# A first MLP whose products go ahead of its transposes, and three zero pieces sent at its end

## The chip, the cores and the metric

The kernel runs on one core of a Trainium2 chip. The metric is the device time of one execution, in microseconds. Engines are named as in the profile: PE (matrix products and transposes; PEld are its weight loads), DVE, ACT and POOL (vector, scalar and general work), SP (which issues most transfers). Sixteen DMA engines move data between the chip's large memory (HBM) and the on-chip memory.

## The reference

Two decoder layers for one token, forward and backward. A layer is an attention part (32 query heads on 4 key/value heads, the last 4096 positions of a cache of 32768) and an MLP with the Mish activation; both layers use the same weights. The result is the output and the gradients of x, both caches, wq, wo, w1, b1 and w2.

```python
x = x + _A_ref(_layernorm(x), k_cache, v_cache, wq, wo)   # A0
x = x + _B_ref(_layernorm(x), w1, b1, w2)                 # B0
x = x + _A_ref(_layernorm(x), k_cache, v_cache, wq, wo)   # A1
x = x + _B_ref(_layernorm(x), w1, b1, w2)                 # B1
# _A_ref: q = x @ wq; softmax(q k^T * Dh**-0.5) v; then @ wo
# _B_ref: h = x @ w1 + b1; act = h * tanh(softplus(h)); act @ w2
_out, _vjp = jax.vjp(_f, x, k_cache, v_cache, wq, wo, w1, b1, w2)
_grads = _vjp(grad_out)
```

Sizes: D = 1024, J = 4096 (wq's columns), F = 3584 (the MLP's width), everything in bf16. The gradients of the caches are zero except in the last 4096 positions, so 58.7 MB of plain zeros have to be written.

## The kernel before, in words

A token's vector lies as columns, 128 elements per column, so a matrix-vector product is a row of PE instructions with a 128x128 block of the weight as the stationary operand and a moving operand of one column. The weights don't fit on the chip at once and are read several times.

**The ring.** Weight chunks of 1 MB go through a ring of eight slots. `ring.want` writes down, in the order of the whole program, which chunk comes next; whenever a slot is released (`ring.release`, after its last reader), `pump` issues the next wanted load on SP (L71). Whoever releases a slot gets not his own next chunk but the next one in the list. In the first layers the list runs: wq, V, w2 chunks 0 and 1, wo, w1, w2 chunks 2 to 6, then wq pieces 0, 1, 2 for layer A1 (pieces 3 to 7 were kept from A0 and hold five slots), wo for A1, wq again, and so on. Chunk 3 of w2 has a home of its own: the tile `zt`.

**Zeros.** `zt` is later set to zero by POOL (L728) and then is the source of 56 zero pieces of 1 MB each, which `zeros(n, after)` issues on POOL's own DMA queue (L264). With `after` given, POOL first copies one element of that tensor (L259), so the pieces start no sooner than it is ready. The places of these calls spread the zeros over the program: nine in A1's forward part, the rest up to the last stage.

**The first MLP, B0** (from L716). After the products with w1 (L621) and the activation on DVE, a loop runs over the seven chunks of w2. `mlp_out` (L673) makes 32 products with AC, the activation. Beside this forward product, each chunk is used for the backward product of the last layer's gradient with w2 (into `da1`), since it is on the chip anyway. Its four blocks of 1024 columns go two ways: blocks 0 and 1 as row products on DVE (`rowdot`, L427; the vector `gbc` broadcast over the partitions), blocks 2 and 3 as `turned`: eight PE transposes into a PSUM buffer (L450), an eviction by ACT back over the block in the ring (L306), and then eight PE products with GB, here called GB products (L462). `later` keeps those back until the next `flush`, so the order on PE is: forward products of chunk c, GB products of chunk c-1, transposes of chunk c. Chunks 0 and 1 were already treated wholly by `rowdot` and are only released.

Chunk 6 has its turn in `last_da`, which is the `q_hook` of A1's `attn_fwd`: it is issued behind the layer norm and ahead of the query product (L493, eight pieces of wq with 32 products each, in the order 3, 4, 5, 6, 7, 0, 1, 2). Behind the query product stand the scores (L510) and the softmax.

**The last stage.** The backward part of A0 (`attn_bwd(0, ...)`) calls the hook `dn1(t)` after each of eight wq pieces. When it is over, the remaining output gradients are made as outer products and written (SP, L989 and L994).

Of the kernel before, what the change touches and what calls it, by code (L numbers as in the profile page):

```python
# [18 lines left out]
D = 1024  # L19
# [4 lines left out]
TD = D // P  # L24
TF = F // P
# [4 lines left out]
def scol(g, t):  # L30
    return ((t // 2) * 4 + g) * 16 + (t % 2) * 8
# [62 lines left out]
def kernel(  # L94
# [22 lines left out]
    nc = tc.nc  # L117
# [13 lines left out]
    def sb(shape, dtype, name):  # L131
        return keep.tile(shape, dtype, name=name)
# [3 lines left out]
    def tmp(shape, dtype, name):  # L136

        if name not in scratch:
            scratch[name] = keep.tile(shape, dtype, name=name)
        return scratch[name]  # L140
# [10 lines left out]
    gbc = DSX[:, 1024:2048]  # L151
# [11 lines left out]
    TP = psum.tile([P, 512], FP32, name="TP")  # L163
# [7 lines left out]
    def big():  # L171
        if wide:
            wide.append(wide.pop(0))
            return wide[-1][:, 0:512]
        b = bigs[big_n[0] % len(bigs)]
        big_n[0] += 1
        return b
# [16 lines left out]
    for hi in range(4):  # L194
        r = slice(32 * hi, 32 * hi + 32)
# [7 lines left out]
    GB = sb([P, TD, 2], BF16, "GB")  # L203
# [16 lines left out]
    ring = Ring(nc, [ring_t[:, i, :] for i in range(8)])  # L220
# [35 lines left out]
    def zeros(n, after=None):  # L256

        if after is not None and zjobs:
            nc.gpsimd.tensor_copy(pz[0:1, pz_n[0] % 16:pz_n[0] % 16 + 1], after[0:1, 0:1])  # L259
            pz_n[0] += 1  # L260
        for _ in range(n):
            if zjobs:
                dst = zjobs.pop()
                nc.gpsimd.dma_start(dst, zt[:])  # L264
# [32 lines left out]
    def evac(dst, src, eng=None, cost=(0.69, 1.0)):  # L297

        if eng is None:
            eng = "D" if load["D"] + cost[0] <= load["A"] + cost[1] else "A"  # L300
        if eng == "D":
            load["D"] += cost[0]
            nc.vector.tensor_copy(dst, src)  # L303
        else:
            load["A"] += cost[1]
            nc.scalar.copy(dst, src)  # L306
# [74 lines left out]
    def residual(y_ps, x, name):  # L381
        xn = sb([P, TD], FP32, f"x_{name}")
        st = tmp([P, 2], FP32, "st")
        junk = tmp([P, TD], FP32, "xx")
        nc.vector.scalar_tensor_tensor(out=xn[:], in0=y_ps, scalar=1.0, in1=x[:], op0=ALU.mult, op1=ALU.add,
                                       accum_out=st[:, 0:1])
        nc.vector.scalar_tensor_tensor(out=junk[:], in0=xn[:], scalar=1.0, in1=xn[:], op0=ALU.mult, op1=ALU.mult,
                                       accum_out=st[:, 1:2])
        return xn, st
# [30 lines left out]
    def rowdot(w, vecs, n, acc, fours=False):  # L420

        for i, vec in enumerate(vecs):
            out, a = junk[:, 0:n], w[:, i * n:(i + 1) * n]
            if fours:
                out, vec = (x.rearrange("a (k p) -> a k p", p=P) for x in (out, vec))
                a = a.rearrange("a (p k) -> a k p", k=4)
            nc.vector.tensor_tensor_reduce(out=out, in0=a, in1=vec, scale=1.0,  # L427
                                           scalar=acc if i else 0.0, op0=ALU.mult, op1=ALU.add, accum_out=acc)
        load["D"] += len(vecs) * (n * 1.1e-3 + 0.18)
# [4 lines left out]
    def later(f, product=False):  # L434

        lag.append((product, f))
        while sum(p for p, _ in lag) > behind[0]:
            lag.popleft()[1]()
        while lag and not lag[0][0]:
            lag.popleft()[1]()  # L440

    def flush():
        while lag:
            lag.popleft()[1]()

    def turned(w, n, mv, eng=None, block=None):

        b = big().bitcast(BF16)
        for i in range(n):
            nc.tensor.transpose(b[:, i * P:(i + 1) * P], block(w, i) if block else w[:, i * P:(i + 1) * P], ident_bf[:])  # L450
        evac(w, b[:, 0:n * P], eng, cost=(0.69 * n / 8, n / 8))
        later(mv, True)

    fresh = [False]

    def mv_open():

        fresh[0] = True

    def mv(w, n, out, rhs_of, last):  # L460
        for i in range(n):
            nc.tensor.matmul(out, lhsT=w[:, i * P:(i + 1) * P], rhs=rhs_of(i), start=fresh[0], stop=last and i == n - 1,  # L462
                             skip_group_check=True)
            fresh[0] = False

    def rows_chunk(ch, c, col, l, vec, dst, off, nr=2, eng="A"):

        for tt in range(4):
            r = 4 * c + tt
            if tt < nr:  # L470
                rowdot(ch[:, tt, :], [vec], D, dst[:, r:r + 1])
            else:
                w = ch[:, tt, :]
                turned(w, TD, lambda w=w, r=r: mv(w, TD, TP[:, off + r:off + r + 1], lambda i: col[:, i, l:l + 1], True), eng)
# [6 lines left out]
    def attn_fwd(l, x, st, first, wo_hook, q_hook=None):  # L481
# [2 lines left out]
        if first:  # L484
            kt_transposes()
        if q_hook is not None:
            q_hook()
        q_ps = MV[:, 0:HQ]
        order = list(range(TD)) if l == 0 else sorted(range(TD), key=lambda t: t not in KEEP_Q)
        for k, t in enumerate(order):  # L490
            ch = ring.get(("q", l, t))
            for h in range(HQ):
                nc.tensor.matmul(q_ps[:, h:h + 1], lhsT=ch[:, h * P:(h + 1) * P], rhs=NA[:, t, l:l + 1],  # L493
                                 start=(k == 0 and h == 0), stop=(k == TD - 1), skip_group_check=True)
            if l == 0 and t in KEEP_Q:
                ring.keep(("q", 0, t), ("q", 1, t))
            else:
                ring.release(("q", l, t))
        qv = QC[:].rearrange("p v (g u l h) -> p v g u l h", g=G, u=2, l=2)
        nc.vector.tensor_scalar(out=qv[:, 0, :, 0, l, :], in0=q_ps.rearrange("p (g h) -> p g h", g=G), scalar1=scale,  # L500
                                scalar2=None, op0=ALU.mult)
# [4 lines left out]
        for i in range(2):  # L506
            for t in range(16 * i, 16 * i + 16):
                for g in range(G):
                    c = scol(g, t) - 512 * i
# [30 lines left out]
        for i in range(2):  # L540
            nc.vector.reduce_sum(m64[i][:], EX[:, i * 512:(i + 1) * 512].rearrange("p (tp c) -> p c tp", c=64), axis=AX.X)
            for g in range(G):
                for t in range(16 * i, 16 * i + 16):
                    c = scol(g, t)
# [22 lines left out]
        y_ps = MV[:, 128:128 + TD]  # L567
        for c in range(8):
            ch = ring.get(("o", l, c))
# [99 lines left out]
    def mlp_out(l, ch, c, y_ps):  # L669
        for tt in range(4):  # L670
            fb = 4 * c + tt
            for dd in range(TD):
                nc.tensor.matmul(y_ps[:, dd:dd + 1], lhsT=ch[:, tt, dd * P:(dd + 1) * P], rhs=AC[:, fb, l:l + 1],  # L673
                                 start=(fb == 0 and dd == 0), stop=(fb == TF - 1), skip_group_check=True)
# [26 lines left out]
    da1 = tmp([P, HQ], FP32, "da")  # L701
    DA = 64
# [13 lines left out]
    mp0 = sB0["deriv"]()  # L716
    y_ps = MV[:, 256:256 + TD]
    mv_open()
    for c in range(7):
        ch = ring.get(("2", 0, c))  # L720
        mlp_out(0, ch, c, y_ps)
        flush()
        if c in EARLY_2:
            ring.release(("2", 0, c))
        elif c < 6:
            rows_chunk(ch, c, GB, 1, gbc, da1, DA)
            later(lambda c=c: ring.release(("2", 0, c)))
    nc.gpsimd.memset(zt[:], 0.0)  # L728
    x2, st2 = residual(y_ps, x1, "B0")


    def last_da():

        rows_chunk(ring.get(("2", 0, 6)), 6, GB, 1, gbc, da1, DA)
        flush()
        ring.release(("2", 0, 6))
        v = da1[:, 8:TF].rearrange("p (a b) -> p a b", b=4)[:, :, 2:4]
        nc.vector.tensor_copy(v, TP[:, DA + 8:DA + TF].rearrange("p (a b) -> p a b", b=4)[:, :, 2:4])

    def wo_hook1(c):  # L740
        if c == 0:
# [15 lines left out]
    def take_back(name, base, off):  # L757
        r = DR[name][:].rearrange("(n l) p -> l n p", l=2)
        nc.sync.dma_start(ROWS[base:base + 2, off:off + r.shape[1] * P].rearrange("l (n p) -> l n p", p=P), r)

    x3, st3, sA1 = attn_fwd(1, x2, st2, False, wo_hook1, last_da)
    put_by("OC", OC, HQ)
    put_by("NA", NA, TD)
# [9 lines left out]
    dnp = sb([P, TD], FP32, "dnp")  # L773
# [231 lines left out]
    def twins():  # L1005
        for base, n in ((96, NOFF + F), (64, NOFF + F), (32, NOFF + J), (0, NOFF + J)):
            nc.sync.dma_start(TWIN[base ^ 32:(base ^ 32) + 2, 0:n], ROWS[base:base + 2, 0:n])
# [26 lines left out]
    def units_cols(base, ncol, out):  # L1034

        for t in range(TD):
            s = stage_free.popleft()
            n = 0
            while n < ncol:
                m = unit_dw(base, t * P, NOFF + 512 * n, s[:, n * 512:ncol * 512], ncol - n)  # L1040
                n += m
                store(out[t * P:(t + 1) * P, :], s, n - m, n, ncol, t == TD - 1)
                yield
# [50 lines left out]
    y_ps = MV[:, 384:384 + TD]  # L1094
    mv_open()
    even()
    for c in range(7):
        ch = ring.get(("2", 1, c))
# [43 lines left out]
        zeros(4, DQC[:, 0, 0:1])  # L1142

    def dn1(t):
        if t in (3, 6, 7):
            zeros(2 if t == 3 else 1, dnp[:, t:t + 1])
        if t == 4:
            twins()
        if t == 5:
            todo[0].append(units_cols(0, 8, out_4))  # L1150
# [57 lines left out]
```

## Time and profile before

| what | value |
|---|---|
| median of 3 runs | 460.42 us (459.21 to 463.47) |
| profiled execution, its own time | 461.23 us |
| its span, first to last instruction | 459.2 us |
| PE busy | 341.7 us (74%) |
| DVE, ACT, POOL busy | 256.6 us (56%), 225.0 us (49%), 38.7 us (8%) |
| moved by DMA | 179.38 MB, 388 GB/s over the span |
| of it on SP's queue, on POOL's queue | 119.74 MB, 58.72 MB |
| mean granted PE clock | 0.629 |

The span is what the profile sees; the execution's own time adds what lies around it, 2.0 us. A PE instruction counts as busy for its whole length although instructions overlap, so a busy PE is not PE at its peak. The granted clock is a share of full speed; it is 0.50 or 1.0 in long stretches of this trace.

### The profile page before, as it was taken

The page shows a single profiled execution, that of the slowest core. Times are in us where ns is not written, and L with a number is a line of the kernel's source. Part 1 is how long each engine was busy: PE and PEld are TensorE (multiplying, and loading weights), DVE is VectorE, ACT ScalarE, POOL GpSimd, SP SyncE. Part 2 cuts the span into 40 slices and gives each one's busy share as a digit, 9 for nine tenths or more (in the row PEclk, how much of TensorE's full clock was granted, in tenths as well). Part 3 has the DMA queues.
Part 4 walks back from the last instruction along what each step waited for, and adds up shares of the span by engine and source line. Part 5 has one row for each costly group of instructions (what it writes and reads, how often), then busy time and mean ns, then how long its engine had stood idle before and what let it go on. Part 6 is the DMA issues. An engine that isn't in the chain of part 4 may idle for free. (4 is left out here: it accounts for less than half of the span.)

```text
span 459.2 us, 14200 instructions
## 1 busy us (share of the span) xinstructions
PE 341.7 (74%) x6361; PEld 276.6 (60%) x6361; DVE 256.6 (56%) x516; ACT 225.0 (49%) x261; POOL 38.7 (8%) x85
## 2 busy tenths in 40 slices
PE   3836445598679888598879798798797888889900
PEld 3735434497569887498779798697693222224600
DVE  4505731283060149677528676657456999998810
ACT  2502001055045379377317555157064999999900
POOL 1000000030103322200211000101221000000000
PEclk9955555555555569699759955589586555555555
DMA  8999999877999999999999988999999999999995
GB/s 337 421 420 418 418 419 416 361 278 261 385 425 422 421 417 418 415 399 415 420 422 418 421 320 298 347 344 368 422 419 424 412 422 422 418 421 416 405 407 213
DMA packets 27802, 179.38 MB, mean 391 GB/s; under 512 B 3642, under 2 KB 3670, under 8 KB 9430
## 3 DMA queue, kind: packets, MB, share of 16 engines
q1 hardware_dynamic: 19586, 119.74, 65.5%
q0 software_dynamic: 8064, 58.72, 30.9%
q8 instruction: 49, 0.80, 0.6%
q14 instruction: 11, 0.09, 0.0%
q10 hardware_dynamic: 92, 0.02, 0.0%
HBM read 79.74 MB, written 98.62 MB: 388 GB/s over the span
## 5 line engine op out<-in xcount | busy, mean ns | idle before, releaser
L306 ACT COPY ring<-BIG 128x1024 bf16<-128x1024 bf16 x62 | 60.7, 1014 | 41.5 <-PE BIG L450 36.1
L450 PE MATMUL BIG<-ident_bf,ring 128*128 128x128 bf16 x744 | 67.4, 255 | 1.8 <-ACT W L306 1.1
L450 PEld LDWEIGHTS <-ring 128*128 128x128 bf16 x816 | 61.5, 116 | 2.8 <-issue 2.2
L1015 PE MATMUL wide<-W 2*128 2x512 bf16 x228 | 52.1, 598 | 9.3 <-ACT W L306 2.0
L427 DVE CUSTOM_DVE_ANT_0 junk<-ring,SC 128x1024 bf16<-128x1024 bf16 x34 | 41.3, 1215 | 5.4 <-DMA ring<-in_B_w_dram 3.7
L1015 PEld LDWEIGHTS <-W 2*128 2x128 bf16 x240 | 12.6, 102 | 44.3 <-issue 43.2
L462 PEld LDWEIGHTS <-ring 128*128 128x128 bf16 x912 | 31.6, 98 | 9.3 <-ACT ring L306 6.7
L306 ACT COPY KT<-BIG 128x1024 bf16<-128x1024 bf16 x22 | 21.8, 1016 | 30.3 <-PE BIG L602 28.7
L303 DVE CAST ring<-wide 128x1024 bf16<-128x1024 f32 (+1 forms) x29 | 33.7, 1199 | 3.2 <-PE wide L1015 1.5
L306 ACT COPY W<-BIG 128x1024 bf16<-128x1024 bf16 x28 | 26.7, 1119 | 16.0 <-PE BIG L788 14.9
L306 ACT CAST ring<-wide 128x1024 bf16<-128x1024 f32 (+1 forms) x35 | 32.9, 1018 | 1.3 <-PE wide L1066 0.5
L303 DVE COPY ring<-BIG 128x1024 bf16<-128x1024 bf16 x31 | 21.3, 690 | 19.3 <-PE BIG L450 12.2
L264 POOL DMA_DIRECT2D out_dram<-zt x56 | 29.7, 534 | 22.9 <-DMA out_dram<-zt 22.0
L621 PE MATMUL MV<-NB,W 128*128 128x1 bf16 x448 | 16.2, 172 | 9.3 <-DMA W<-in_B_w_dram 6.5
L493 PE MATMUL MV<-NA,ring 128*128 128x1 bf16 x512 | 14.9, 165 | 11.0 <-DMA ring<-in_A_wq_dram 8.6
L621 PEld LDWEIGHTS <-W 128*128 128x128 bf16 x448 | 15.9, 118 | 9.8 <-DMA W<-in_B_w_dram 7.2
L303 DVE CAST VS<-wide 128x1024 bf16<-128x1024 f32 (+1 forms) x17 | 19.7, 1186 | 3.6 <-PE wide L1015 3.0
L1066 PE MATMUL wide<-W 32*128 32x256 bf16 x128 | 20.9, 402 | 0.9 <-ACT ring L306 0.8
L306 ACT CAST KT<-wide 128x1024 bf16<-128x1024 f32 x20 | 20.4, 1032 | 1.8 <-PE wide L1015 0.9
L493 PEld LDWEIGHTS <-ring 128*128 128x128 bf16 x512 | 14.2, 103 | 11.5 <-DMA ring<-in_A_wq_dram 9.1
L427 DVE CUSTOM_DVE_ANT_0 junk<-ring,DSX 128x1024 bf16<-128x1024 bf16 x16 | 19.6, 1224 | 1.1 <-DMA ring<-in_B_w_dram 0.7
L427 DVE CUSTOM_DVE_ANT_0 junk<-W,SC 128x512 bf16<-128x512 bf16 (+1 forms) x20 | 15.8, 791 | 6.5 <-PE SC L330 5.8
(268 smaller groups left out, 566.9 us busy)
## 6 DMA issues: line engine op xcount, KB each, us to landing
out_dram<-zt POOLq DMA_DIRECT2D x56, 1024.0 KB, 16.2
ring<-in_A_wq_dram SPq DMA_DIRECT2D x22, 1024.0 KB
ring<-in_A_wo_dram SPq DMA_DIRECT2D x14, 1024.0 KB
ring<-in_B_w_dram SPq DMA_DIRECT2D x13, 1024.0 KB
W<-in_A_wo_dram SPq DMA_DIRECT2D x10, 1024.0 KB
W<-in_B_w_dram SPq DMA_DIRECT2D x8, 896.0 KB
out_dram<-ring SPq DMA_DIRECT2D x7, 1024.0 KB
out_dram<-ring SPq DMA_DIRECT2D x13, 512.0 KB
```

The costliest lines, as they stand in the source:

```text
L264: nc.gpsimd.dma_start(dst, zt[:])
L303: nc.vector.tensor_copy(dst, src)
L306: nc.scalar.copy(dst, src)
L427: nc.vector.tensor_tensor_reduce(out=out, in0=a, in1=vec, scale=1.0, scalar=acc if i else 0.0, op0=ALU.mult, op1=ALU.add, accum_out=acc)
L450: nc.tensor.transpose(b[:, i * P:(i + 1) * P], block(w, i) if block else w[:, i * P:(i + 1) * P], ident_bf[:])
L462: nc.tensor.matmul(out, lhsT=w[:, i * P:(i + 1) * P], rhs=rhs_of(i), start=fresh[0], stop=last and i == n - 1, skip_group_check=True)
L493: nc.tensor.matmul(q_ps[:, h:h + 1], lhsT=ch[:, h * P:(h + 1) * P], rhs=NA[:, t, l:l + 1], start=(k == 0 and h == 0), stop=(k == TD - 1), ...
L621: nc.tensor.matmul(h_ps[:, fb:fb + 1], lhsT=f_block(W1[:, t], fb), rhs=NB[:, t, l:l + 1], start=(t == 0 and fb == 0), stop=(t == TD - 1), ...
L1015: nc.tensor.matmul(b[:, 512 * i:512 * i + 512], lhsT=R[at:at + 2, lo:lo + P], rhs=R[at:at + 2, ro + 512 * i:ro + 512 * i + 512], start=Tru ...
L1066: nc.tensor.matmul(b[:, k * 256:(k + 1) * 256], lhsT=RT[32 * g:32 * g + 32, a, tp, :], rhs=YS[32 * g:32 * g + 32, :], start=True, stop=Tru ...
```

## The change

In B0 the loop over the chunks is written out by hand. `turned` is split into `turn_pe` (the transposes) and `turn_ev` (the eviction), so that the two can stand at different places. The transposes of chunk 2 are issued ahead of the first forward products; evictions and GB products of a chunk follow later, with forward products of the next chunk between them. Chunk 5's and chunk 6's transposes, evictions and GB products move into the second query product: `q_hook` is now called with -1 ahead of it and with k behind each of its eight pieces, and `last_da` acts at -1, 1 and 3. Right behind the memset of `zt`, three zero pieces are issued on POOL. In the last stage `dn1` issues one piece instead of four: one at t = 3 instead of two, none at t = 6 and 7. The number of pieces, 56, and all arithmetic stay.

```diff
+    def turn_pe(w, n, block=None):
         b = big().bitcast(BF16)
         for i in range(n):
             nc.tensor.transpose(b[:, i * P:(i + 1) * P], block(w, i) if block else w[:, i * P:(i + 1) * P], ident_bf[:])
+        return b
+
+    def turn_ev(w, b, n, eng=None):
         evac(w, b[:, 0:n * P], eng, cost=(0.69 * n / 8, n / 8))
+
+    def turned(w, n, mv, eng=None, block=None):
+        turn_ev(w, turn_pe(w, n, block), n, eng)
         later(mv, True)
...
         if q_hook is not None:
-            q_hook()
+            q_hook(-1)
...
+            if q_hook is not None:
+                q_hook(k)
...
-    for c in range(7):
-        ch = ring.get(("2", 0, c))
-        mlp_out(0, ch, c, y_ps)
-        flush()
+    def da_out(c):
+        mlp_out(0, ring.get(("2", 0, c)), c, y_ps)
+    def da_dots(c):
+        ch = ring.get(("2", 0, c))
+        for tt in range(2):
+            rowdot(ch[:, tt, :], [gbc], D, da1[:, 4 * c + tt:4 * c + tt + 1])
+    def da_turn(c):
+        ch = ring.get(("2", 0, c))
+        held[c] = [(ch[:, tt, :], turn_pe(ch[:, tt, :], TD)) for tt in (2, 3)]
+    def da_put(c):
+        for w, b in held[c]:
+            turn_ev(w, b, TD, "A")
+    def da_mv(c):
+        for tt, (w, _) in zip((2, 3), held.pop(c)):
+            r = DA + 4 * c + tt
+            mv(w, TD, TP[:, r:r + 1], lambda i: GB[:, i, 1:2], True)
+        ring.release(("2", 0, c))
+
+    da_turn(2)
+    for c in range(3):
+        da_out(c)
         if c in EARLY_2:
             ring.release(("2", 0, c))
-        elif c < 6:
-            rows_chunk(ch, c, GB, 1, gbc, da1, DA)
-            later(lambda c=c: ring.release(("2", 0, c)))
+    da_put(2)
+    da_dots(2)
+    da_out(3)
+    da_turn(3)
+    da_put(3)
+    da_dots(3)
+    da_mv(2)
+    da_out(4)
+    da_mv(3)
     nc.gpsimd.memset(zt[:], 0.0)
+    zeros(3)
+    da_turn(4)
+    da_put(4)
+    da_dots(4)
+    da_out(5)
+    da_dots(5)
+    da_mv(4)
+    da_out(6)
     x2, st2 = residual(y_ps, x1, "B0")
-    def last_da():
-        rows_chunk(ring.get(("2", 0, 6)), 6, GB, 1, gbc, da1, DA)
-        flush()
-        ring.release(("2", 0, 6))
-        v = ...
+    def last_da(k):
+        if k == -1:
+            da_turn(5)
+            da_put(5)
+            da_dots(6)
+        elif k == 1:
+            da_mv(5)
+            da_turn(6)
+            da_put(6)
+        elif k == 3:
+            da_mv(6)
+            v = ...
...
     def dn1(t):
-        if t in (3, 6, 7):
-            zeros(2 if t == 3 else 1, dnp[:, t:t + 1])
+        if t == 3:
+            zeros(1, dnp[:, t:t + 1])
```

## The prediction

> **What bounds the kernel now.** I read the page first, then the chain that ended last, then tables by stretches around the edit and at the end, then the timeline there, and last the packet and landing records of the trace. The page says which resource is full:
>
> ```profile
> DMA  8999999877999999999999988999999999999995
> GB/s 337 421 420 418 418 419 416 361 278 261 385 425 422 421 417 418 415 399 415 420 422 418 421 320 298 347 344 368 422 419 424 412 422 422 418 421 416 405 407 213
> ```
>
> A slice is 11.5 us. The DMA engines are full but for two holes, slices 7 to 10 (80 to 126 us, where the diff works) and 23 to 27 (264 to 321 us). The end is a drain: the last instruction of any compute engine starts at 437.04, and the span ends at 459.2.
>
> ```profile
> 433.57 0.87 DVE KT L303
> ...
> 437.04 1.21 DVEq L1203
> ```
>
> ```profile
> 90.00:96.00 6.00, 5.53 (x154) 5.45 (x154) 5.66 (x18) 1.93 (x2) 0.00 (x0) 0.50 0.70 246
> 96.00:102.00 6.00, 5.88 (x120) 5.79 (x121) 5.24 (x9) 3.43 (x4) 2.30 (x1) 0.50 0.79 318
> 102.00:108.00 6.00, 5.75 (x104) 5.59 (x101) 1.97 (x12) 4.58 (x6) 1.21 (x1) 0.50 0.66 195
> 108.00:114.00 6.00, 3.95 (x135) 3.61 (x134) 2.57 (x6) 2.62 (x4) 0.00 (x0) 0.50 0.69 243
> 114.00:120.00 6.00, 3.66 (x138) 3.60 (x136) 0.00 (x0) 0.00 (x0) 0.00 (x0) 0.50 1.02 419
> ...
> 440.00:450.00 10.00, 0.00 (x0) 0.00 (x0) 0.00 (x0) 0.00 (x0) 0.00 (x0) 0.50 1.02 407
> ```
>
> Read the last two columns: DMA share and GB/s. From 90 to 108 PE is full at clock 0.50 and DMA is not; from 114 on DMA is full again. At 440 to 450 nothing computes and DMA is full. So the time is the moment at which the stores can begin (355.5), plus the stores' bytes over about 415 GB/s; before that moment the program runs at PE's pace, with a few waits for loads. Two things can move the end: a shift of the compute chain before 355.5, and what stands in the DMA engines when the stores begin.
>
> **The tail: three zero pieces leave t = 3, 6, 7.**
>
> ```profile
> 344.14 1.05 POOL L264 DMA_DIRECT2D out_dram<-zt  x2
> ...
> 348.81 0.53 POOL L264 DMA_DIRECT2D out_dram<-zt  x1
> ...
> 350.08 0.53 POOL L264 DMA_DIRECT2D out_dram<-zt  x1
> ```
>
> ```profile
> 355.53 1.90 SPq L994 DMA_DIRECT2D out_dram<-VS  x2
> ```
>
> Three pieces are 3.15 MB, 7.6 us at 415 GB/s, and it is tempting to take 7.6 us off a drain. But the stores start only when the units after the last layer norm have run (355.53, SP), and PE sets that. The packets show the zero queue empty on nearly all engines at 358.5, the first store packets at 356.5. Without three of its last fourteen pieces the queue is empty at about 350.5, and DMA then idles until 356.5. What is gained is only the overlap of zeros and stores: summed over the packets after 356.4, about 1.3 us for a mean engine, and about 2.6 us for the one engine that lags (a piece issued last lands there at 362.0, on the fifteenth of the sixteen at 359.0). That engine lands the last store too, 458.2 against 455.1. I take **-2.2**, bounds -1.3 and -3.1. The two marker copies of POOL that go too (L259, 0.2 us each) stood in its idle time.
>
> The Trainium skill (DMA: Bandwidth & Descriptors, "Latency and other measured facts") says that two engines are usually slower and puts this, as a guess, to descriptors written by software, as POOL's zero pieces are. By that rule the whole lag would go with the pieces, and the tail would give -3.1 instead of -2.2. The trace shows one such engine.
>
> **First MLP.** Before, its order is:
>
> ```profile
> 90.35 2.70 PE L673 MATMUL MV<-AC,ring 128*128 128x1 bf16 x96 [2.41 <-DVE AC L648]
> 91.37 5.35 SPq L71 DMA_DIRECT2D ring<-in_B_w_dram  x3
> 92.91 1.87 PE L450 MATMUL BIG<-ident_bf,ring 128*128 128x128 bf16 x16
> 99.70 3.51 POOL L728 MEMSET zt<- 128x4096 bf16 x1 [63.65 <-PE TP L462]
> 102.92 8.54 SPq L71 DMA_DIRECT2D ring<-in_A_wq_dram  x3
> 105.45 0.17 DVE L385 SCALAR_TENSOR_TENSOR x_B<-MV,x_A 128x8 f32<-128x8 f32 x1 [2.81 <-PE MV L673]
> ```
>
> A chunk's products are 0.87 us, its 16 transposes 1.66 until the next instruction, its two GB products 0.71, its two evictions on ACT 1.93. da_turn(2) is put ahead of da_out(0) and would fill PE's 2.41 us wait for AC. It can't: chunk 2 lands at 90.53 by the landing records, 0.2 us after AC is ready. So it runs from 90.6, with all of PE's queue behind it, and da_out(0) starts at 92.3, +1.9; the releases of chunks 0 and 1, and so the loads of 4 and 5, go from 91.4 and 92.2 to 93.3 and 94.1. Then on PE: products 0, 1, 2 to 94.9, product 3 to 95.8, turning 3 to 97.4, GB products 2 to 98.1; chunk 2's release, the load of chunk 6, at 98.4 against 96.4. Its landing moves with it from 102.5 to 104.4. Meanwhile products 4, GB products 3 (99.8, so the memset stays at about 99.9), turning 4, products 5, GB products 4 end at 103.4. PE then waits a microsecond for chunk 6, and the residual comes at 105.5: **0.0**, bounds -1.4 (chunk 6 not late: products 6 end at 104.3 less the DVE step) and +1.
>
> **Second query product.** Before, 110.92 to 120.36, with a hole that is no load:
>
> ```profile
> 110.92 5.79 PE L493 MATMUL MV<-NA,ring 128*128 128x1 bf16 x212
> ...
> 119.05 1.31 PE L493 MATMUL MV<-NA,ring 128*128 128x1 bf16 x44 [2.34 <-issue]
> ...
> 124.97 1.32 PE L510 MATMUL SC<-QC,KT 128*128 128x8 bf16 x44 [1.95 <-issue]
> ```
>
> Both "issue" holes end just after a 16 KB packet of the instruction queue (116.78 and 122.71 in the packet records): PE has run out of instructions while DMA is full. After: turning 5 in the layer norm's shadow to 108.3, then eight products of 0.87, GB products 5 and 6 (1.4), turning 6 (1.66), 0.3 of wait for ACT: 118.7 without holes. (The copy out of TP at k = 3 makes DVE wait for GB products 6 until some 115; behind it stands only the copy to QC, due at 120.) But the loads move. q(1,1) and q(1,2) are no longer released by chunks 5 and 6 (106.2, 111.1) but by query pieces 3 and 4, at 109.3 and 110.2. And the three zero pieces, issued on POOL at 103.5 behind the memset (nothing else of POOL's waits behind them before 120), reach the engines some 3.5 us later (137.68 to 140.74 and 288.70 to 292.95 in the trace), at 107. From then DMA is full. Where both queues had work, 128 to 136 us, each had 0.5 of the engines; so q(1,1) and q(1,2), 2.1 MB at 210 GB/s from 110.2, end at 120 and land at 121 to 122, against 116.2 now. The product ends at 121.9 to 122.9. The first instruction hole lies inside this wait, and the second shrinks from 1.95 to about 0.7, since its block is asked for while PE waits: the SC products end at 126.5 to 127.2 against 126.3. The eight o loads behind them are 5 us later; o7 lands at about 150 against 144.2, and is used at 149.0. Together **+1.0**, bounds -1.7 (118.7 for 120.36) and +3.5 (q at 123, o7 1.5 late).
>
> **What the zeros displace.** Between 88 and 112 DMA idles about 2.5 us less than before, on the lagging engine too; three pieces cost it 8.0 us (one per 2.65 us while the queue ran alone). So some 4.5 us of zeros, with 1.0 of shift taken off, are still ahead at each later point until a hole takes them. The queue next empties in the second MLP's backward part, where loads are needed at once:
>
> ```profile
> 276.59 1.01 PE L673 MATMUL MV<-AC,ring 128*128 128x1 bf16 x32 [0.93 <-DMA ring<-in_B_w_dram]
> ```
>
> ```profile
> 276.68 1.22 DVE L427 CUSTOM_DVE_ANT_0 junk<-ring,SC 128x1024 bf16<-128x1024 bf16 x1 [3.31 <-DMA ring<-in_B_w_dram]
> ```
>
> Chunk 4 lands there at 276.5, the last zero at 277.2, both last on the lagging engine; chunks 5 and 6 follow at full rate, 279.5 and 282.0, just as they are used (279.55, 282.86). With 4.5 us of zeros left, chunk 5 takes two shares, +2.4, and chunk 6 some +1 more. PE is the chain here, and nothing until 355.5 gives it back. **+2.4**, bounds 0 (backlog gone by then) and +3.4.
>
> **Sum.** -2.2 + 0.0 + 1.0 + 2.4 = +1.2 on the profiled execution's 461.2 (span 459.2 and 2.0 around it), 462.4. The median of the runs, 460.4, lies 0.8 lower; against it I forecast **461.8**, with a range of its own from 460 to 464.
>
> **The rivals.**
> *The contention does not bite.* Zeros and loads share, but q and o land before use and the later backlog is gone by 270. Then the tail stays, -2.2, and the two instruction holes shrink: between -2.2 and -2.2 - 1.7 = -3.9, so 456.5 to 458.2. For it: o loads have 7 to 17 us of slack except the last. Against: q(1,2) is wanted at 117.8 and has 2.1 MB of zeros beside it.
> *The early zeros are paid twice* (the slower side): the price is set on the lagging engine, at q(1,2) (+2.6), o7 (+1.5) and chunks 5 and 6 (+3.4), with a tail of only -1.3: +6.2, 466.6. It decides from the point where the zero queue still holds more than one piece (2.65 us) when chunk 5 is asked for. For it: chunk 4 waits so already. Against: from 276 to 288 the DMA share is 0.86 to 0.92, so a backlog has some room to run off.
> *It doesn't do what it says.* The turnings and zeros only change places and the two shifts cancel: 460.4.
>
> **How the numbers follow.** Forecast 0.50, no contention 0.27, paid twice 0.15, nothing 0.08. A measurement of this kernel tells about 1% (4.6 us) from no change. Faster by more (under 455.8): 0.08, the part of the first rival that goes 0.7 past its far end. Slower by more (over 465.0): 0.11 from paid twice and 0.03 from the forecast. The rest, 0.78, lies within. Cases of both signs hold the chance, so the range for 8 in 10 goes from 457.5 to 466.5.
>
> **What would show it.** Right, if after: da_out(0)'s row starts near 92.3, with the L450 row ahead of it at 90.6; the residual stays within 1 us of 105.5; L493's wait names a DMA load; zeros appear on POOL at about 103.5; the MLP rows near 280 wait longer for in_B_w; DMA share falls below 1 between 350 and 356; the first store is issued 2 to 5 us later than 355.5, and the span between it and the end is 2 us shorter than 103.7. Wrong, if the first store comes earlier than 355, or if the stretch from it to the end shrinks by over 4 us, for then the zeros did hold back the drain.

## The result, and the profile after

The changed kernel takes 462.44 us (median), against 460.2 for the kernel before measured beside it: a ratio of 1.0043, with a 95% interval of 1.0030 to 1.0056. By this ratio it is slower by 2.0 us (0.43% of 460.2; the medians differ by 2.2), less than a measurement of this kernel was expected to resolve and, over twenty runs of each, resolved all the same. The forecast was 461.8.

The two profiled executions don't show those 2 us between them: 461.06 us after (span 459.3) and 461.23 before (span 459.2). One execution of this kernel strays by a microsecond or two: the profiled one after is 1.4 us below the median of its runs, the one before 1.0 above. So the stages are read first and the sum is made afterwards, with further profiles of the same stages.

First the page of the kernel after, its DMA share and rate in slices of 11.5 us:

```profile
DMA  8999999868999999999999997799999699999998
GB/s 337 420 420 418 419 419 417 360 274 300 422 424 423 420 420 425 417 414 402 419 425 415 421 416 290 274 352 365 411 420 383 263 412 418 412 422 413 407 407 324
```

The first hole has become shorter: slice 10 gives 422 GB/s where it gave 385. The second begins a slice later: slice 23 still has 416 GB/s, where it had 320. And there is a new hole in slices 30 and 31 (383 and 263 GB/s), just ahead of the stores. The zeros have been carried from the end through the whole program.

The same table by stretches as before (PE, PEld, DVE, ACT, POOL busy, clock, DMA share, GB/s):

```profile
90.00:96.00 6.00, 5.45 (x148) 5.45 (x149) 5.69 (x17) 1.19 (x2) 0.00 (x0) 0.50 0.31 104
96.00:102.00 6.00, 4.53 (x92) 4.45 (x91) 3.25 (x6) 2.87 (x4) 1.01 (x1) 0.50 1.00 408
102.00:108.00 6.00, 4.43 (x98) 4.18 (x97) 3.22 (x12) 3.30 (x5) 4.23 (x4) 0.50 0.59 172
108.00:114.00 6.00, 5.48 (x133) 5.40 (x131) 3.01 (x7) 4.61 (x6) 0.00 (x0) 0.50 0.98 388
114.00:120.00 6.00, 3.31 (x125) 3.23 (x122) 0.17 (x1) 0.59 (x1) 0.00 (x0) 0.50 1.01 423
...
350.00:356.00 6.00, 4.99 (x105) 3.20 (x102) 4.94 (x15) 2.56 (x6) 0.00 (x0) 0.59 0.85 353
356.00:362.00 6.00, 4.41 (x21) 1.00 (x21) 3.26 (x5) 5.31 (x10) 0.00 (x0) 0.50 0.32 129
```

DMA lies idle from 90 to 96 (0.31; before 0.70), because the loads of chunks 4 and 5 are asked for later, and is full from 96 to 102. From 102 to 108 PE has 4.43 us of work where it had 5.75. At the end the share falls to 0.85 and 0.32, where before it was 1.00 and 1.01: the zeros no longer cover the last units.

The timeline after, where the diff works, then the second MLP's backward part and the first store (start, duration, engine or queue, line, operation; in brackets the wait ahead of it and what ended it):

```profile
90.56 1.89 PE L450 MATMUL BIG<-ident_bf,ring 128*128 128x128 bf16 x16 [2.75 <-DMA ring<-in_B_w_dram]
92.24 2.75 PE L682 MATMUL MV<-AC,ring 128*128 128x1 bf16 x96
93.31 5.07 SPq L71 DMA_DIRECT2D ring<-in_B_w_dram  x3
99.44 1.01 PE L682 MATMUL MV<-AC,ring 128*128 128x1 bf16 x32 [1.47 <-DMA ring<-in_B_w_dram]
104.81 1.73 POOL L264 DMA_DIRECT2D out_dram<-zt  x3 [0.31 <-POOL zt L766]
106.17 0.17 DVE L385 SCALAR_TENSOR_TENSOR x_B<-MV,x_A 128x8 f32<-128x8 f32 x1 [1.61 <-PE MV L682]
119.95 1.01 PE L500 MATMUL MV<-NA,ring 128*128 128x1 bf16 x32 [2.69 <-DMA ring<-in_A_wq_dram]
123.81 1.01 PE L500 MATMUL MV<-NA,ring 128*128 128x1 bf16 x32 [2.84 <-DMA ring<-in_A_wq_dram]
125.10 3.55 PE L519 MATMUL SC<-QC,KT 128*128 128x8 bf16 x128 [0.28 <-DVE QC L509]
153.62 1.01 PE L582 MATMUL MV<-OC,ring 128*128 128x1 bf16 x32 [1.60 <-DMA ring<-in_A_wo_dram]
...
278.35 1.22 DVE L427 CUSTOM_DVE_ANT_0 junk<-ring,SC 128x1024 bf16<-128x1024 bf16 x1 [2.78 <-DMA ring<-in_B_w_dram]
283.42 1.22 DVE L427 CUSTOM_DVE_ANT_0 junk<-ring,SC 128x1024 bf16<-128x1024 bf16 x1 [2.58 <-DMA ring<-in_B_w_dram]
288.20 1.22 DVE L427 CUSTOM_DVE_ANT_0 junk<-ring,SC 128x1024 bf16<-128x1024 bf16 x1 [2.29 <-DMA ring<-in_B_w_dram]
...
359.39 0.82 SPq L1047 DMA_DIRECT2D out_dram<-VS  x2
```

PE's wait of 2.4 us ahead of the first products is still there, now 2.75 and ended by a load: the transposes put there did not fill it, they took its place. Two waits for wq stand in the query product, where before one hole without a load stood. In the second MLP chunks 4, 5 and 6 are all waited for, where before it was mainly 4 (3.31 us, and 0.44 for 5). The first store goes out at 359.39 instead of 355.53.

Six moments of the chain, in us from the start of each span, show where it slipped. "Again" is a second profile of the kernel before. g2 is the gradient that goes into the second MLP's backward part, dh0 the one that this part leaves behind; each is marked by its cast on DVE. The query product's copy carries its result to QC.

| kernel | B0 residual | query product's copy | second attention's residual | g2 cast | dh0 cast | first store | store to end |
|---|---|---|---|---|---|---|---|
| before | 105.45 | 120.40 | 150.58 | 261.99 | 288.43 | 355.53 | 103.67 |
| before, again | 105.29 | 119.80 | 150.26 | 261.42 | 287.40 | 355.43 | 101.56 |
| after | 106.17 | 124.85 | 154.76 | 264.35 | 293.33 | 359.39 | 99.88 |
| zeros_only | 105.54 | 123.01 | 153.22 | 265.25 | 292.25 | 359.78 | 99.85 |
| order_only | 105.34 | 120.01 | 151.03 | 262.50 | 288.60 | 356.39 | 101.18 |
| behind_query | 105.73 | 120.29 | 152.46 | 262.93 | 292.61 | 360.38 | 99.90 |
| held_back | 105.31 | 124.94 | 154.08 | 262.80 | 288.04 | 354.10 | 100.48 |
| late_hole | 105.21 | 120.39 | 151.62 | 262.51 | 288.34 | 357.82 | 99.87 |
| two_in_hole | 105.27 | 119.80 | 150.54 | 261.18 | 287.50 | 354.54 | 99.88 |
| turn_late_hole | 104.99 | 119.74 | 151.01 | 261.32 | 287.47 | 354.61 | 99.90 |
| turn_late_hole_2 | 104.49 | 119.24 | 151.08 | 263.20 | 288.87 | 356.80 | 99.87 |
| turn_late_two | 104.86 | 119.48 | 150.23 | 260.63 | 287.15 | 354.60 | 99.89 |

The last column but one plus the last is the span. How far one profile can be trusted is seen from the two pairs of equal kernels: before and its repetition differ by up to 1.0 us ahead of the first store, turn_late_hole and turn_late_hole_2 by up to 2.2.

### The profile page after: what moved, and what is told of

Its sections match the earlier page's. It is cut to its first block, busy times and chain, and to the rows that moved or that the text cites. A ratio compares the mean times of both kernels' runs of the same rounds, so it can differ in the third digit from the quotient of the medians.

```text
span 459.3 us, 14200 instructions
## 1 busy us (share of the span) xinstructions
PE 340.0 (74%) x6361; PEld 274.7 (60%) x6361; DVE 256.6 (56%) x516; ACT 224.7 (49%) x261; POOL 38.3 (8%) x83
## 3 DMA queue, kind: packets, MB, share of 16 engines
q1 hardware_dynamic: 19586, 119.74, 64.9%
## 5 line engine op out<-in xcount | busy, mean ns | idle before, releaser
L450 PE MATMUL BIG<-ident_bf,ring 128*128 128x128 bf16 x744 | 67.1, 254 | 5.1 <-DMA ring<-in_B_w_dram 2.8
L306 ACT COPY KT<-BIG 128x1024 bf16<-128x1024 bf16 x22 | 21.7, 1018 | 29.0 <-PE BIG L611 27.3
L264 POOL DMA_DIRECT2D out_dram<-zt x56 | 29.7, 534 | 30.8 <-DMA out_dram<-zt 29.7
```

## The experiments

The theory to be tested was that of the prediction: the products' new order is worth about nothing by itself; the three early pieces cost time twice, beside the second query product's loads and, as a backlog in the queues, beside the second MLP's; and taking them out of the last stage gives about 2 us back. The rivals put the loss on the order, or on one of the two places alone, or deny the gain at the end.

**zeros_only: the pieces without the order.** Before, with the three pieces moved.

```diff
     nc.gpsimd.memset(zt[:], 0.0)
+    zeros(3)
...
-        if t in (3, 6, 7):
-            zeros(2 if t == 3 else 1, dnp[:, t:t + 1])
+        if t == 3:
+            zeros(1, dnp[:, t:t + 1])
```

> The zeros' half of the change alone, in the order of before. Theory (the zero pieces displace loads, the tail gives some 3.8 us back): chunk products and the residual stay where they were (105.4); q(1,2), issued at 111.1, shares the DMA engines with the pieces and lands at 117.5 instead of 116.2, the query product ends at 120 to 122; o7 of wo and chunks 5 and 6 of the second MLP come late by 1.5 and 3 us; first store at 359 to 360, 100 us from there to the end: 460 to 462 in all, no change. Rival (the new order alone costs the time, the zeros cost nothing): first store at 355.5, the end at 455.4: 456 to 457, faster.

Measured: 1.0006 [0.9978, 1.0033]. PE waits for wq here too, in the timeline of zeros_only:

```profile
117.12 0.69 PE L493 MATMUL MV<-NA,ring 128*128 128x1 bf16 x20 [0.84 <-DMA ring<-in_A_wq_dram]
121.96 1.01 PE L493 MATMUL MV<-NA,ring 128*128 128x1 bf16 x32 [2.93 <-DMA ring<-in_A_wq_dram]
```

The copy behind the product comes 2.6 us late, at 123.0 where 120 to 122 was expected, the first store 4.3, and the drain is 99.85: a loss and a gain of some 2 to 4 us each, which cancel within the interval. So the time alone says little about a moved transfer; the moments of the chain say more.

**order_only: the order without the pieces.** After, with the pieces where they were before.

```diff
     nc.gpsimd.memset(zt[:], 0.0)
-    zeros(3)
...
-        if t == 3:
-            zeros(1, dnp[:, t:t + 1])
+        if t in (3, 6, 7):
+            zeros(2 if t == 3 else 1, dnp[:, t:t + 1])
```

> The new order alone, with the zero pieces where they were. Theory: da_out(0) starts at 92.2 and the residual comes at 106.2 (+0.7); q(1,1) and q(1,2), issued at 109.8 and 110.6 with the DMA engines to themselves, land at 114 and 117, the query product ends at 119 to 121; nothing is late at o7 or in the second MLP; first store at 355.5 to 357, 103.7 us from there to the end: 460 to 462. Rival (the order is what costs): query product end at 124 again, first store at 359, and the old tail: 464 to 465.

Measured: 0.9999 [0.9977, 1.0020]. Every moment up to the first store lies within 0.9 us of before, and no load of the query product is waited for: the two last wq pieces land at 113.79 and 116.27, where after they land at 119.90 and 123.76. The residual was expected at 106.2 and comes at 105.34. What is left in its query product is the hole named "issue", 1.69 us. The order alone costs and brings nothing that shows.

Neither half costs anything measurable; together they cost 0.43%. That the halves need each other for it is not shown: the interval of zeros_only reaches 0.33%, that of the change begins at 0.30%, and the chain of zeros_only is as late at the first store (359.78) as that of after (359.39). The packets do show a way in which the halves meet inside the query product. In the new order the loads of q(1,1) and q(1,2) go out at 109.8 and 110.6, just behind the zeros' first packets (109.1); in zeros_only q(1,1) goes out at 106.3, ahead of them, and only one of the two loads is badly late.

**behind_query: all five pieces behind the query product.** It takes the contention out of that place alone and leaves the backlog.

```diff
-            zeros(2)
+            zeros(5)
...
     nc.gpsimd.memset(zt[:], 0.0)
-    zeros(3)
```

> After, but with the three early pieces issued with the two that stand behind the second query product (zeros(5) there). Theory: the query product ends at 119 to 121 instead of 124.7, since its loads have the engines alone; but the pieces then stand beside the wo loads (o6 and o7 late by 2 to 3 us) and the backlog at the second MLP's chunks 4 to 6 stays, as late as in after: first store at 358 to 360, 100 us to the end: 459 to 461. Rival (the query product's wait is the whole cost): first store at 355.5, 456 to 457.

Measured: 1.0049 [1.0019, 1.0079]: as slow as the change. The query product's copy is back at 120.29, so its 4.5 us are indeed the zeros' doing. But the last o load is then late (PE waits 1.28 us for it in the timeline, the residual is at +1.9), and from g2 to dh0 it takes 29.7 us as after takes 29.0, against 26.4 and 26.0 in the two profiles of before. DVE's waits there are 4.24, 1.59 and 2.61. The first store comes at 360.38, a little later than expected (358 to 360). Clearing the first place gains nothing in the end: what is saved there is lost later.

**held_back: the pieces early, the backlog cleared.** After, with three pieces that were issued ahead of the second MLP's backward part, two in the stage before it (`dn3`) and one at g2, held back until dh0.

```diff
-        if t in (3, 5):
-            zeros(1, dnp[:, t:t + 1])
...
-    zeros(1, g2)
-    zeros(2, dh0)
+    zeros(5, dh0)
```

> After, with three pieces that before and after issue around 250 to 265 (two in the backward part of A1 at t = 3 and 5, one behind g2) held back to where two pieces already stand, behind dh0. Theory (chunks 4, 5 and 6 of the second MLP wait for zeros still queued): the queue of zeros is empty before chunk 4 is asked for, the DVE waits there (2.78, 2.58 and 2.29 us in after) go to under 1 us together, dh0 comes 26 us after g2 as in before and not 29; first store 2 to 4 us earlier than 359.4 unless five pieces behind dh0 delay the wo loads: 458.5 to 460.5. Rival (those waits come from something else, the shifted clock windows or the later issue of the loads): dh0 stays 29 us behind g2 and the end at 462.

Measured: 0.9943 [0.9916, 0.9970], faster than before by 2.6 us, and with 457.98 us a little faster than expected. It keeps the late query product (124.94) and loses what comes after it. Its only wait of DVE for the MLP's chunks in the timeline:

```profile
274.80 1.22 DVE L427 CUSTOM_DVE_ANT_0 junk<-ring,SC 128x1024 bf16<-128x1024 bf16 x1 [0.98 <-DMA ring<-in_B_w_dram]
```

2.78 + 2.58 + 2.29 us have become 0.98, and g2 to dh0 takes 25.2 us. The stretch just before, 264 to 270, of held_back, of before and of after:

```profile
264.00:270.00 6.00, 5.88 (x125) 5.80 (x123) 5.83 (x10) 3.28 (x4) 0.00 (x0) 0.50 0.41 132
264.00:270.00 6.00, 5.88 (x124) 5.80 (x121) 5.83 (x11) 3.66 (x4) 0.00 (x0) 0.50 0.84 314
264.00:270.00 6.00, 5.29 (x113) 5.22 (x114) 5.11 (x10) 1.93 (x2) 0.71 (x2) 0.65 1.01 422
```

The DMA share is 0.41, 0.84 and 1.01. The packets give the size of the backlog. Of the zeros issued by 270 us, what is still to be moved when g2 is cast is 0.13 MB in held_back, 1.32 in both profiles of before, 1.74 in zeros_only, 2.13 in after and 3.86 in behind_query; and from g2 to dh0 these take 25.2, 26.4 and 26.0, 27.0, 29.0 and 29.7 us, which is the same order. So the backlog, not the loads' own order, makes the second MLP wait. Before itself has some of it, so that held_back gains there as well. It also suggests that the query product's loss is not what decides: a chain that is 4.5 us late at 125 is 0.8 late at 262.

**late_hole: the pieces in the hole behind the second MLP's loads.** Before's order; the three pieces are sent at chunk 5 of the last MLP loop, when no load of that MLP is to follow.

```diff
         rows_chunk(ch, c, GB, 0, LB[0], da0, DA)
+        if c == 5:
+            zeros(3, da0[:, 20:21])
...
-        if t in (3, 6, 7):
-            zeros(2 if t == 3 else 1, dnp[:, t:t + 1])
+        if t == 3:
+            zeros(1, dnp[:, t:t + 1])
```

> Before, but with the last stage's three pieces (one of two at t = 3, those at t = 6 and 7) issued behind chunk 5's row products of the second MLP's backward part, at about 281, when chunk 6 is landing and the DMA engines are not full. Theory (what the tail gives is real, what the early place costs is the place): everything up to 288 as before, loads of wo behind it have 6 to 10 us of slack, first store at 355.5 to 356.5, 100 us from there to the end: 456 to 457.5, ratio 0.992. Rival (three pieces cost their 8 us wherever loads run): the wo loads between 297 and 306 come late by 3 us or more, first store at 359, no gain: 460.

Measured: 0.9953 [0.9926, 0.9981]. Up to dh0 the chain is that of before, and the drain is 99.87. The gain at the end is thus real; what it needs is a place for the pieces where nothing waits for a load. The profile's first store, 357.82, is later than expected (355.5 to 356.5) and than in the kernels with the same hole below, and the trace doesn't show a wait that accounts for all of it.

**two_in_hole: only two of the three leave the end.**

```diff
+        if c == 5:
+            zeros(2, da0[:, 20:21])
...
-        if t in (3, 6, 7):
-            zeros(2 if t == 3 else 1, dnp[:, t:t + 1])
+        if t == 3:
+            zeros(2, dnp[:, t:t + 1])
```

> Before, with two pieces at 281 instead of late_hole's three, so that the last stage keeps two at t = 3. Theory (only what still stands in the queue when the first store starts costs time; the queue of twelve pieces is empty at 353): the same end as late_hole, first store to end 99.9 to 100.5, 456.5 to 457.5. Rival (each piece taken from the last stage gives 1.2 us): 458.

Measured: 0.9941 [0.9903, 0.9978], drain 99.88. The third piece is worth nothing in the drain, as the stretch after already says, where DMA idles (0.32) between 356 and 362: the drain's floor is the stores alone, some 99.9 us.

**before_again: the kernel before, unchanged**, for the scatter of its drain.

> Before itself, profiled once more, to see how much of a stage's length is scatter. If the stretch from the first store to the end belongs to the kernel, it is 103.7 us again; if a part is scatter of the lagging DMA engine, between 101 (as in order_only, whose last stage is the same) and 103.7.

One execution of 458.76 us. Its chain reaches the first store at 355.43, 0.1 us from the first profile, but the drain is 101.56 instead of 103.67. With order_only, whose last stage is before's, there are three profiles of it: 103.67, 101.56, 101.18, mean 102.1. The first profile has the longest end of the three, which between them differ by 2.5 us.

**turn_late_hole: the order mended, and the hole.** order_only, with chunk 2's transposes behind the first three products, its GB products ahead of chunk 3's transposes, and late_hole's pieces.

```diff
-    da_turn(2)
     for c in range(3):
         da_out(c)
         ...
+    da_turn(2)
     da_put(2)
     da_dots(2)
     da_out(3)
+    da_mv(2)
     da_turn(3)
     da_put(3)
     da_dots(3)
-    da_mv(2)
     da_out(4)
```

> The new order with chunk 2's transposes behind the forward products of chunks 0 to 2 instead of ahead of them, and chunk 2's GB products ahead of chunk 3's transposes; the three pieces at 281 as in late_hole. Theory (the transposes ahead cost 1.9 us because chunk 2 lands at 90.5): the first forward product starts at 90.3, loads of chunks 4 to 6 go at 91.3, 92.2 and 96.5, the residual comes at 104.3 to 104.6, the query product ends a microsecond before order_only's 119.9; with the tail of late_hole 456 to 457.5. Rival (the residual waits for chunk 6 whatever the order, or PE's instruction holes take the microsecond back): query product at 120, 457.4 as late_hole.

Measured: 0.9893 [0.9855, 0.9931]; 455.89 us, just under the 456 to 457.5 expected. The products start at 90.41 as before the change, and the residual comes at 104.99, 1.2 us ahead of after; the query product's copy, expected a microsecond ahead of order_only's, is 0.3 ahead. The same kernel under a second name:

> turn_late_hole once more, beside turn_late_two on one chip, since its first comparison rested on few runs: 455.5 to 457, ratio 0.990 to 0.994.

Measured: 0.9918 [0.9894, 0.9943]; 455.34 us. And with two pieces in the hole instead of three, two staying at t = 3:

```diff
-            zeros(3, da0[:, 20:21])
+            zeros(2, da0[:, 20:21])
...
-            zeros(1, dnp[:, t:t + 1])
+            zeros(2, dnp[:, t:t + 1])
```

> The order of turn_late_hole (chunk 2's transposes behind the forward products) with two pieces at 281 as in two_in_hole. If the two gains are of different places and add up: two_in_hole's 0.994 with the order's 0.5 us on top, 456 to 457; if turn_late_hole's 455.9 was the order, the same 455.9; first store to end 99.9 in any case.

Measured: 0.9925 [0.9912, 0.9938]; 456.22 us, the same as its neighbour. These are some 4 us below the kernel before, and some 6 below the changed one. How much of that is the mended order and how much the hole is not settled: the intervals of two_in_hole and late_hole overlap theirs. One profile strays by half of that: turn_late_hole_2 has its first store at 356.80, 2.2 us later than the other two.

## Why the prediction was right, step by step

**The kind of limit** held. The end is the first store plus a drain: all profiles with three or two pieces fewer in the last stage, but for held_back, have a drain of 99.85 to 99.90, whatever happened before it.

**The tail**, -2.2 with bounds -1.3 and -3.1: in the two profiles of before and after it is 103.67 - 99.88 = -3.8, outside the bounds, and by the prediction's own words close to the figure (4) that would have made it wrong. With the further profiles it is 102.1 - 99.9 = -2.2, the mean of -3.8, -1.7 and -1.3. The sum of the packets after 356.4 was a sound way to the size; that it was met to the tenth, with three profiles so far apart, is luck. The Trainium skill's guess (DMA: Bandwidth & Descriptors, "Latency and other measured facts"), by which the lag of the slow engine goes with the software-written descriptors, fits what was seen: the last of the last store's sixteen parts lands 3.1, 1.9 and 0.9 us after the fifteenth in the three profiles with zeros beside the stores, and 0.1 to 0.4 in the ones without (0.9 in held_back). The rule pointed the right way; its sum of -3.1 took the longest lag of the three for the usual one.

**The first MLP**, 0.0: the steps came to within 0.4 us. The transposes at 90.56 (90.6 expected), the first product at 92.24 (92.3), the loads of chunks 4, 5 and 6 at 93.31, 94.16 and 98.05 (93.3, 94.1, 98.4). The residual is at +0.72, inside the bounds, because chunk 6 landed at 105.07 instead of 104.4; in order_only it landed at 104.25, in held_back, whose first MLP is after's, at 104.22, and the residual at -0.1 in both. So the 0.7 belongs to this one profile. One wait was overlooked: chunk 4, asked for 1.9 us later, lands at 99.39 and costs PE 1.47 us, which is why memset and zeros ran a microsecond later than worked out.

**The second query product**, +1.0 with bounds -1.7 and +3.5, is the term that was mis-sized. The mechanism was right: both queues' packets share the engines from 113 on. Here are both queues between 104 and 128 us, first of before, then of after (packets, MB, share of the engines):

```profile
q1 hardware_dynamic: 1028, 7.52, 83.8%
q0 software_dynamic: 65, 0.53, 5.3%
```

```profile
q1 hardware_dynamic: 785, 5.78, 63.1%
q0 software_dynamic: 432, 3.15, 31.4%
```

The 3.15 MB of zeros pass there, and the loads' queue moves 1.74 MB less. The product was to end 1.5 to 2.5 us later; it ended 4.45 later, 3.7 of it in the product itself. The step that failed is "2.1 MB at 210 GB/s from 110.2": it gave the loads their half from the moment of issue. By the packet records the load issued at 109.78 got its first packets at 113.4, 3.6 us later, where the load issued at 93.31, with no zeros beside it, got them after 1.0. From 110.3 to 113.3 the loads' queue moves nothing, and it has about half of the engines only from 114. (The zeros' own first packets came at 109.1, not at 107.) So the last wq piece landed at 123.76, not at 121 to 122. The shrinking hole was underrated too: it vanished (128 score products in one row), so that the scores end only 2.4 us late (128.65 against 126.29), where +0.2 to +0.9 was expected. The last o load then made PE wait 1.60 us; the residual comes 4.2 us late.

**What was given back** had no term in the sum. Of those 4.2 us, 2.4 are left at g2, and held_back keeps 0.8 of its 3.5; but the 2.6 of zeros_only become 3.3. Of after's part one item is seen: before has a hole of 1.63 us in PE's transposes of KT (L602) ahead of 164.05 (1.35 in its second profile), which the trace puts down to ACT, with an instruction packet at 161.76; after's packet comes at 164.26 and no hole follows. The stage as a whole, from the residual to g2, takes 111.4 and 111.2 us in the two profiles of before and 109.6 in after, but 110.3 and 112.1 in the two of one kernel, turn_late_hole. So the 1.8 us may be scatter, and what else pays stays open. Between dh0 and the first store, after regains 1.0 more, where the prediction held of the second MLP's loss that nothing until 355.5 gives it back. This isn't shown to be the change's either: the stage takes 67.1 and 68.0 us before, 66.1 in after and in held_back, and up to 69.5 (late_hole).

**The second MLP**, +2.4 with bounds 0 and +3.4: g2 to dh0 grew from 26.4 to 29.0 us, +2.5, and the new waits are those for chunks 5 and 6, as forecast. The experiments show the cause: the stage lengthens with the zeros still queued at its start and shortens when the queue is emptied ahead of it (held_back). Two things were otherwise than worked out. DMA was to idle some 2.5 us less from 88 to 112 than before; over the four stretches from 90 to 114 it worked 17.0 us before and 17.3 after, because the later loads of chunks 4 and 5 left idle about as much as the zeros filled. And the price isn't a fixed one. In zeros_only, after and behind_query g2 comes 3.3, 2.4 and 0.9 us behind before, and dh0 3.8, 4.9 and 4.2 behind: the less a chain has lost until g2, the more it waits there. So the two places don't simply add, as the sum took them to, and how close +2.5 comes to +2.4 is in part luck.

**The sum**: +0.7 until the B0 residual, +3.5 until the second attention's, -1.8 until g2, +2.5 until dh0, -1.0 until the first store, together +3.9 where +3.4 was predicted; with -2.2 for the drain, +1.7. The ratio of the runs says +2.0, but after's profiled execution is 1.4 us below its median, and no profile shows where these 1.4 are. Some +2.5 us more in the query product than predicted, and -2.8 of what came back without a term, nearly cancelled. So the total was met partly by luck; the mechanism, early zeros that delay loads at both places and a tail that gives only part of it back, was right.

## What to carry to other kernels

Where the DMA engines are full, a transfer sent early does not vanish. Here 3.15 MB sent at 105 us left 1.0 MB more to be moved at 264 us than before (2.18 MB for 1.14). So look for the next place where a load is used as soon as it lands, and price the transfer there; a chain that is already late waits less there. Send such work just behind the last load that anyone waits for (with the order of before, 1.0006 for zeros_only became 0.9953 for late_hole), and only as much as overlaps with the end. Work that is moved into an engine's wait must have its own operand by then: the wait of 2.4 us ahead of the first products could not be filled, because the chunk to be turned landed as it ended.

## What the runs showed of the hardware that was not expected

PE's holes named "issue" in the query product and the scores (1.6 to 3.0 us, each behind a 16 KB packet of the instruction queue, with DMA full and products of one or eight columns running) are not a fixed cost. In after, where PE waits for loads at that time, they are gone, in zeros_only and held_back 0.8 and 1.4 us of them remain there; so they pay back part of such a wait: about 2 us in the scores here, where the prediction counted on 1.25. That PE had run out of instructions is inferred from the order of the records.

A newly issued load can wait long for its first packet beside a queue that is already running: 3.6 us in after beside the zeros, 1.0 without them.

A clock of 1.0 comes in stretches that are multiples of 3.41 us: 10.2, 17.1, 27.3, 20.5, 20.5 and 10.2 us in the profile of before, 10.2, 20.5, 27.3, 20.5, 20.5 and 10.2 after. The Trainium skill (TensorE: Matmul & The Clock Gate, "Part 1: The HAM clock gate") tells of a free-running window of 3413 ns, and the traces agree. A stage can gain or lose one window without any change of the kernel: the second stretch is 17.1 us in the first profile of before and 20.5 in the second. What such a window is worth in time no run here measures.
